# Spacing the weight buffers of parts 2 and 3 over 512 bytes (attention with sinks, then mixture of experts, fp32, one core)

## The chip, the cores and the metric

The kernel runs on one core of one Trainium2 chip. The metric is the time on the device in microseconds. The kernel before takes 2079.2 us, the median of 2 runs (2079.17 and 2079.23).

## The reference, cut to what matters

Attention with 4 sink tokens and a window of 128 gives `x` (3072 tokens, 512 wide). Then come 8 experts: two dense layers with a ReLU between them, and the sum over the experts, weighted by a matrix `P` that a few Sinkhorn steps make from a gate. Nearly all of the arithmetic is in the two products of the loop.

```python
def _moe_ref(x, w_gate, w1, w2):          # x 3072x512, w1 8x512x1024, w2 8x1024x512
    ...
    for e in range(E):
        h = np.maximum(x @ w1[e], 0.0)
        ye = h @ w2[e]
        out += P[:, e:e + 1] * ye
    return out.astype(np.float32)
```

## The kernel before

**Parts and units.** After the attention the 3072 tokens are worked through in three parts of 1024. The code counts them 0, 1, 2; parts 2 and 3 of the title are `part` 1 and 2, and they run the same code. A part goes over 32 units: 8 experts times 4 slices of 256 hidden columns (`units1`).

**Products.** fp32 values are split into a high and a low fp32r half, and three of the four cross products are kept. On top of that both layers use a fast matrix scheme with seven products M1 to M7 in place of eight, for which each unit's weights are kept in DRAM as seven ready "forms" (`w1s`, `w2s`), written during part 1. In parts 2 and 3 a unit's first layer is seven products of 6 matmuls each (`product`, L902: `c<-B,W1q` or `c<-T,W1q`). Its second layer takes units in pairs: 14 groups of 6 matmuls for a pair of units, one group a tick (L1467: `o<-hf,W2q` or `held<-hf,W2q`); in such a group a buffer of `W2q` is read by 3 matmuls in a row, in a product a buffer of `W1q` by 6. So a unit is 42 + 42 = 84 matmuls, all with 128x128 stationary weights and 512 moving columns.

**What is stationary, what moves.** In each matmul the stationary operand is 128 columns of a weight form, 512 bytes of a partition, out of a buffer `W1q` or `W2q`. The moving operand is 2048 bytes of a partition: of `XF` (the token forms B11 to T4) in the first layer, of `hf` (the hidden forms) in the second.

**Buffers and loads.** `W1q` has 8 buffers and `W2q` 16 (`W1N`, `W2N`), each 2048 bytes a partition, one form per buffer, used in turn. `load_w1` (L1350 to L1356) and `load_w2` (L1370 to L1376) put one DMA per form on SP's queue: 128 rows of 2048 bytes. A buffer is asked for again one tick after the last matmul that read it. The first four forms of part 2 come out of another pool (`WT`, `early_form`) and are no part of the change. Pools hand out addresses one buffer after the other, and in the built program all buffers named here begin at a multiple of 512 bytes: the `W1q` buffers at 76800, 78848, 80896 and so on, those of `W2q` from 196096 on, and all of `XF` and `hf` too.

**What sets the order.** The program stands in the order in which it is written (`manual_schedule`). `tick` runs what is due and then one product or one group of the second layer; `STEPS2` is the order of ticks in a unit.

Of the kernel before, what the change touches and what calls it, by code (L numbers as in the profile page):

```python
# [10 lines left out]
F32R = mybir.dt.float32r  # L11
# [5 lines left out]
P = 128  # L17
# [221 lines left out]
def tile_sink_attention_moe(ctx: ExitStack, tc: tile.TileContext, q, k, v, wg, w1, w2, out):  # L239
# [15 lines left out]
    KH = KC // 2  # L255
# [7 lines left out]
    def f32(ap):  # L263
        return ap.bitcast(F32)
# [118 lines left out]
    for hh in range(2):  # L383
        t = att2.tile([P, NP, CW + 2 * P], F32, name=f"KQF{hh}")
# [520 lines left out]
    HD = DM // 2  # L905
    weighted = []
    W1Q = {}
# [34 lines left out]
    w1p, cp, rawp, sp, xrp = (pool_(*a) for a in (("w1p", 1), ("cp", 1), ("rawp0", 2), ("sp", 2), ("xrp", 1)))  # L942
# [393 lines left out]
    with ExitStack() as p1:  # L1336
        pool_ = lambda name, bufs, **kw: p1.enter_context(tc.tile_pool(name=name, bufs=bufs, reuse_waits="tile", **kw))
        W1N, W2N = 8, 16
        w1p, pb, cp, wp, hp = pool_("w1q", W1N), pool_("pb", 2), pool_("cq", 1), pool_("wq", 6), pool_("hq", 16)
        ORDER = ["M2", "M1", "M5", "M3", "M6", "M7", "M4"]  # L1340
        units1 = [(e, u) for e in range(E) for u in range(NU)]
        NJ = len(units1)
# [3 lines left out]
        W2Q = {}  # L1346
        coming1 = iter([(part, n, m) for part, n in jobs1 for m in ORDER if (part, n, m) not in W1Q])
        first_ones = set(W1Q)

        def load_w1(k):  # L1350
            for _ in range(k):
                key = next(coming1, None)
                if key:
                    part, n, m = key
                    t = W1Q[key] = w1p.tile([P, 2, KH, P], F32R, name="W1q")
                    nc.sync.dma_start(f32(t).rearrange("p w k f -> p w (k f)"), w1s[units1[n]][:, FA[W1_OF[m]]])  # L1356

        W2_OF = {"M1": "B11", "M2": "B21", "M3": "B22", "M4": "T4", "M5": "T1", "M6": "T2", "M7": "T3"}
# [11 lines left out]
        def load_w2(k):  # L1370
            for _ in range(k):
                key = next(coming2, None)
                if key:
                    part, n, m = key
                    t = W2Q[key] = w2p.tile([P, 2, HD], F32R, name="W2q")
                    nc.sync.dma_start(f32(t), w2s[units1[n]][:, FORMS.index(W2_OF[m])])  # L1376

        PBS = {}
# [13 lines left out]
        def first2(part, n):  # L1392
# [4 lines left out]
            def run(m):  # L1397
                c = "c2" if m in ("M2", "M5", "M3") else "c1"
                start = m in ("M2", "M1", "M5")
                if start:  # L1400
                    T[c] = ps0.tile([P, HT], F32, name=c)
                W = W1Q.pop((part, n, m))
                product(T[c], lambda a, k: W[:, a, k, :], XF[READS[m]], start, True)
                if (part, n, m) not in first_ones:
                    at(1, lambda: load_w1(1))
                if (part, n) == (1, NJ - 1):
                    at(1, lambda: load_form(m))
# [48 lines left out]
        def second2(part, group):  # L1456

            begin, end = group[0] == 0, group[-1] == NJ - 1
            for m, k in order_of(group):
# [11 lines left out]
                def then(m=m, k=k, o=o, hold=hold):  # L1471
                    if hold:
                        sums[m, k] = o
                    elif end and (m, k) == ("M3", 1):
                        for cols in HALVES if part == 2 else (slice(0, HT),):
                            nc.vector.tensor_add(sums["M6", k][:, cols], o[:, cols], sums["M6", k][:, cols])
                    elif begin:
                        t = sums[m, k] = (accq if (m, k) in FEW else accp).tile([P, DM], F32, name="acc")
                        nc.scalar.copy(t, o)
                    else:  # L1480
                        nc.vector.tensor_add(sums[m, k], o, sums[m, k])  # L1481
                    if end:
                        together(part, m, k)
                        if (m, k) == ("M4", 1):
                            at(2 if part == 2 else 3, lambda: put_out(part, 1))
                        if part == 1 and (m, k) == ("M3", 1):
                            at(2, lambda: put_out(part, 0))
                        if part == 2 and m in ("M2", "M3"):

                            d = 2 * (m == "M3") + k  # L1490
                            at(1 if d == KC - 1 else 2, lambda d=d: last_out(d, ("c1", "c2", "held1", "held3")[d]))
                    if (m, k) != ("M3", 1) and k == 1 or (m, k) == ("M3", 0) and not end or (m, k) == ("M3", 1) and end:
                        at(1, lambda: load_w2(len(group)))
# [92 lines left out]
        def second_pools():  # L1586
            nonlocal w2p, accq
            p0r.close()
            w2p, accq = pool_("w2q", W2N, side="right"), pool_("accq", 3, side="right")
            load_w2(W2N)  # L1590

        w2p = accq = None
        load_weights(1, 0)
        load_w1(W1N)
        unit(1, 0, last_second, BEGIN[0])
        unit(1, 1, last_second, BEGIN[1][:-1] + [second_pools] + BEGIN[1][-1:])
# [46 lines left out]
```

## Time and profile before

| | |
|---|---|
| median of 2 runs | 2079.2 us |
| span of the profiled execution | 2077.3 us, so 1.9 us of the time lie outside it |
| PE (TensorE matmul) busy | 2060.9 us, 99% |
| PEld (TensorE weight load) busy | 1706.0 us, 82%, beside the matmuls |
| DVE, ACT, POOL busy | 70%, 40%, 34% |
| chain that ended last | 96% PE |
| granted TensorE clock | 0.999 of full speed, mean of the span |
| DMA | 453.78 MB moved, queue q1 busy for 69.6% of 16 engines' span |
| matmuls of `W1q` and `W2q` | 2664 and 2688 |

The page gives an engine's busy time, and for each group of instructions the line, the engine, what is written and read, the count and the mean duration. A matmul's duration there (389 ns for 512 columns) is longer than its share of the time, since matmuls overlap; the spacing of starts in the timeline is what counts. A row of the timeline merges neighbours of one line and gives the first one's start and the time from that start to the last one's end.

### The profile page before, as it was taken

How to read it: one execution, taken by the hardware profiler on the slowest of the kernel's cores; microseconds unless marked ns; L12 is line 12 of the kernel's file. 1: busy time of each engine (PE TensorE's matmuls, PEld its weight loads, DVE VectorE, ACT ScalarE, POOL GpSimd, SP SyncE). 2: the span in 40 equal slices, each digit the busy share in tenths (PEclk: the TensorE clock that was granted, in tenths of full speed). 3: DMA queues.
4: the chain of work that ended last, by engine and by line, in shares of the span. 5: the costliest groups of instructions: out<-in, count | busy, mean ns of one | idle time of the engine just before them, and what ended most of it. 6: DMA issues, size and time to landing. Idle time of an engine off the chain costs nothing.

```text
span 2077.3 us, 31257 instructions
## 1 busy us (share of the span) xinstructions
PE 2060.9 (99%) x10407; PEld 1706.0 (82%) x10407; DVE 1462.4 (70%) x2732; ACT 840.2 (40%) x1787; POOL 713.7 (34%) x833
## 2 busy tenths in 40 slices
PE   8999999999999999999999999999999999999998
PEld 7888778888888888888888888888888888888887
DVE  6777688787877767756666666666666667666666
ACT  7877445444444444333323322332432232333222
POOL 7766523333333321322322232233332223222323
PEclk9999999999999999999999999999999999999999
DMA  7655269898989886766666666668766666666662
GB/s 178 161 118 120 85 211 323 288 319 291 315 282 323 289 274 223 280 211 197 199 203 198 204 205 191 202 207 334 224 208 194 200 205 191 207 203 202 197 193 83
DMA packets 397622, 453.78 MB, mean 218 GB/s; under 512 B 99664, under 2 KB 265744, under 8 KB 396560
## 3 DMA queue, kind: packets, MB, share of 16 engines
q1 hardware_dynamic: 397064, 451.57, 69.6%
q8 instruction: 85, 1.39, 0.3%
q14 instruction: 81, 0.66, 0.1%
q10 hardware_dynamic: 392, 0.16, 0.0%
HBM read 314.17 MB, written 137.46 MB: 217 GB/s over the span
## 4 chain that ended last, share of the span: by engine, by line
PE 96%; DVE 2%; ACT 1%; POOL 0%; issue 0%; DMA 0%; SPq 0%; DVEq 0%; ACTq 0%; POOLq 0%
PE c L902 42%; PE o L1467 21%; PE held L1467 8%; PE held L1152 7%; PE o L1152 7%; PE st L638 2%; PE st L652 2%; PE st L572 2%; PE st L498 2%; PE st L457 1%; PE st L530 1%; PE st L580 0%; DVE sc L508 0%; DVE st L507 0%; PE st L603 0%
## 5 line engine op out<-in xcount | busy, mean ns | idle before, releaser
L928 ACT CAST hf<-w 128x512 fp32r<-128x512 f32 x448 | 265.3, 621 | 562.2 <-POOL w L1434 299.7
L1467 PE MATMUL o<-hf,W2q 128*128 128x512 f32 x1920 | 472.0, 389 | 0.0
L1467 PEld LDWEIGHTS o<-hf,W2q 128*128 128x128 f32 x1920 | 360.0, 188 | 75.5 <-DVE acc L1481 0.9
L902 PE MATMUL c<-T,W1q 128*128 128x512 f32 x1530 | 388.8, 389 | 0.2 <-DVE w L1415 0.2
L931 DVE TENSOR_TENSOR hf<-w,hf 128x512 fp32r<-128x512 f32 x448 | 329.1, 763 | 75.6 <-ACT hf L928 68.0
L902 PEld LDWEIGHTS c<-T,W1q 128*128 128x128 f32 x1530 | 286.8, 188 | 60.7 <-DVE w L1415 0.9
L1481 DVE TENSOR_TENSOR acc<-o,acc 128x512 f32<-128x512 f32 x298 | 204.6, 687 | 169.9 <-PE o L1467 169.9
L902 PE MATMUL c<-B,W1q 128*128 128x512 f32 x1134 | 278.3, 389 | 0.0
L1434 POOL TENSOR_TENSOR w<-w 128x512 f32<-128x512 f32 x64 | 82.7, 1293 | 492.0 <-DVE w L1416 492.0
L902 PEld LDWEIGHTS c<-B,W1q 128*128 128x128 f32 x1134 | 212.5, 188 | 44.0
L1415 DVE TENSOR_TENSOR w<-c,M 128x512 f32<-128x512 f32 x192 | 132.2, 689 | 139.9 <-PE c L902 135.6
L1411 ACT COPY M<-c 128x512 f32<-128x512 f32 x192 | 112.8, 587 | 249.1 <-PE c L902 249.0
L1467 PE MATMUL held<-hf,W2q 128*128 128x512 f32 x768 | 194.8, 389 | 0.0
L1152 PE MATMUL held<-W2f,h 128*128 128x512 f32 x672 | 171.1, 390 | 0.0
L902 PE MATMUL c<-T,W1f 128*128 128x512 f32 x672 | 171.0, 390 | 0.1
L1152 PE MATMUL o<-W2f,h 128*128 128x512 f32 x672 | 170.5, 389 | 0.1
L1467 PEld LDWEIGHTS held<-hf,W2q 128*128 128x128 f32 x768 | 144.0, 188 | 29.8
L1449 POOL TENSOR_TENSOR w<-w 128x512 f32<-128x512 f32 x64 | 106.3, 1661 | 176.0 <-DVE hf L931 176.0
L1152 PEld LDWEIGHTS o<-W2f,h 128*128 128x128 f32 x672 | 126.0, 188 | 27.0 <-DVE acc L1159 0.9
L902 PEld LDWEIGHTS c<-T,W1f 128*128 128x128 f32 x672 | 125.8, 188 | 26.9 <-issue 0.5
L1152 PEld LDWEIGHTS held<-W2f,h 128*128 128x128 f32 x672 | 125.8, 188 | 26.4 <-DVE W2f L931 0.5
L961 POOL TENSOR_TENSOR r<-r 128x256 f32<-128x256 f32 x27 | 20.1, 745 | 367.8 <-ACT M L1115 231.4
(216 smaller groups left out, 2740.3 us busy)
## 6 DMA issues: line engine op xcount, KB each, us to landing
W2q<-w2s SPq DMA_DIRECT2D x448, 256.0 KB, 3.1
W1q<-w1s SPq DMA_DIRECT2D x444, 256.0 KB, 2.8
w1s<-W1f SPq DMA_DIRECT2D x56, 896.0 KB, 7.7
w2s<-WT SPq DMA_DIRECT2D x136, 256.0 KB, 3.2
r<-in_moe_w_dram SPq DMA_DIRECT2D x64, 512.0 KB, 5.5
w2s<-W2f SPq DMA_DIRECT2D x56, 256.0 KB, 5.7
PB<-psd SPq DMA_DIRECT2D x16, 512.0 KB, 4.0
w2s<-W2f SPq DMA_DIRECT2D x56, 128.0 KB, 7.8
```

Of the source, the lines that this page charges most:

```text
L498: nc.tensor.matmul(ps[hh * HH + 2 * pr + r][:, 0:w], lhsT=Q[rows, a, pr, :], rhs=K[rows, c, pr, 0:w], start=(j == 0), stop=(j == len(terms ...
L572: nc.tensor.matmul(O[r * D:(r + 1) * D, c], lhsT=x_[:, 2 * c + r], rhs=y_[:, 2 * c + r], start=(j == 0 and c == 0), stop=(j == len(ops) - ...
L902: nc.tensor.matmul(ps, lhsT=w1(a, k), rhs=x[:, b, k, :], start=(start and j == 0), stop=(stop and j == len(TERMS) - 1), skip_group_check=n ...
L928: nc.scalar.copy(dst[:, 0], src)
L931: low_ = nc.vector.tensor_sub(dst[:, 1], src, f32(dst[:, 0])).ins
L1152: nc.tensor.matmul(o, lhsT=h[c, th][:, a, off:off + P], rhs=W2F[n][:, w, c, :], start=(begin and c == 0 and j == 0), stop=(end and c == 1 ...
L1411: nc.scalar.copy(t, T["c2"])
L1415: nc.vector.tensor_add(w, T["c1"], T[m])
L1434: nc.gpsimd.tensor_sub(S3, T["A11"], T["A21"])
L1449: at(k, lambda: nc.gpsimd.tensor_sub(T["A11"], w, T["A11"]))
L1467: nc.tensor.matmul(o, lhsT=W2Q[part, n, m][:, a, k * P:(k + 1) * P], rhs=F[part, n, H_OF[m]][:, w, :], start=(j == 0 and (begin or not hol ...
L1481: nc.vector.tensor_add(sums[m, k], o, sums[m, k])
```

## The change

Each of the two pools now hands out tiles that are longer than what is used: by 16 words (64 bytes) for `W1q` and by 8 words (32 bytes) for `W2q`. The form lies in the first 2048 bytes, and the rest is never touched. As the tiles follow each other, the eight `W1q` buffers begin at 0, 64, 128, ... 448 modulo 512 bytes, and the sixteen `W2q` buffers at 0, 32, 64, ... 480. The pools behind them move by 512 bytes in all, so `XF`, `hf` and the other tiles stay at multiples of 512.

```diff
+        def spaced(pool, gap, name):
+
+            return pool.tile([P, 2 * HD + gap], F32R, name=name)[:, 0:2 * HD]
+
...
-                    t = W1Q[key] = w1p.tile([P, 2, KH, P], F32R, name="W1q")
+                    t = W1Q[key] = spaced(w1p, 16, "W1q").rearrange("p (w k f) -> p w k f", w=2, k=KH)
                     nc.sync.dma_start(f32(t).rearrange("p w k f -> p w (k f)"), w1s[units1[n]][:, FA[W1_OF[m]]])
...
-                    t = W2Q[key] = w2p.tile([P, 2, HD], F32R, name="W2q")
+                    t = W2Q[key] = spaced(w2p, 8, "W2q").rearrange("p (w d) -> p w d", w=2)
                     nc.sync.dma_start(f32(t), w2s[units1[n]][:, FORMS.index(W2_OF[m])])
```

No instruction is added, taken away or moved on any engine; the lines behind the new function have numbers larger by 5. Since the pools' ends move by up to 512 bytes, a few of the first loads into fresh buffers wait for other instructions than before. On SP's queue, at the start of part 2, the load of the expert weights `PB` stands ahead of the first eight loads of `W1q`:

```order
 L1205 DMA WT<-w1s_4750 128x512 [waits DMAHW5_49,PE_49]
 L1205 DMA WT<-w1s_4750 128x512 [waits DMAHW6_49]
-L1383 DMA PB<-psd 128x1024 [waits DMAHW7_49,DVE_49]
-L1356 DMA W1q<-w1s_4750 128x512 [waits DMAHW0_49,PE_49]
-L1356 DMA W1q<-w1s_4750 128x512 [waits DMAHW1_49]
...
+L1388 DMA PB<-psd 128x1024 [waits DMAHW7_49,DVE_49,PE_49]
+L1361 DMA W1q<-w1s_4750 128x512 [waits DMAHW0_49,PE_49]
+L1361 DMA W1q<-w1s_4750 128x512 [waits DMAHW1_49]
```

The load of `PB` waits for a count of PE too now. In the built program that count is 2067, and the load of `W1q` right behind it in the same queue waits for 4359, before and now.

## Rows read from the trace of the kernel before

**Rows 1.** The page: span, busy time by engine, granted clock, chain by engine.
```profile
span 2077.3 us, 31257 instructions
...
PE 2060.9 (99%) x10407; PEld 1706.0 (82%) x10407; DVE 1462.4 (70%) x2732; ACT 840.2 (40%) x1787; POOL 713.7 (34%) x833
...
PEclk9999999999999999999999999999999999999999
...
PE 96%; DVE 2%; ACT 1%; POOL 0%; issue 0%; DMA 0%; SPq 0%; DVEq 0%; ACTq 0%; POOLq 0%
```

**Rows 2.** Chain in order of time, part 2: start, length, engine, line, count.
```profile
900.19 4.08 PE c L902 x18
919.23 4.08 PE c L902 x18
```

**Rows 3.** Waits of PE from 860 us on: total, times, longest.
```profile
PE c L902 <- DVE w L1415: 0.2, 1, 0.2
```

**Rows 4.** Stretch 900 to 1400 us: busy time by engine, clock, DMA share, GB/s.
```profile
900.00:1400.00 500.00, 500.00 (x2207) 414.02 (x2206) 339.28 (x500) 152.78 (x264) 146.33 (x105) 1.00 0.66 201
```

**Rows 5.** Page, groups of matmuls: line, out<-in, count | busy us, mean ns | idle.
```profile
L1467 PE MATMUL o<-hf,W2q 128*128 128x512 f32 x1920 | 472.0, 389 | 0.0
...
L902 PE MATMUL c<-T,W1q 128*128 128x512 f32 x1530 | 388.8, 389 | 0.2 <-DVE w L1415 0.2
...
L902 PE MATMUL c<-B,W1q 128*128 128x512 f32 x1134 | 278.3, 389 | 0.0
...
L1467 PE MATMUL held<-hf,W2q 128*128 128x512 f32 x768 | 194.8, 389 | 0.0
```

**Rows 6.** Timeline of matmuls, part 3: start, length, line, out<-in, count.
```profile
1602.34 1.52 PE L902 MATMUL c<-T,W1q 128*128 128x512 f32 x6
1603.70 1.52 PE L1467 MATMUL held<-hf,W2q 128*128 128x512 f32 x6
```

**Rows 7.** Timeline of weight loads at the same place, part 3.
```profile
1602.11 1.32 PEld L902 LDWEIGHTS c<-T,W1q 128*128 128x128 f32 x6
1603.47 0.64 PEld L1467 LDWEIGHTS held<-hf,W2q 128*128 128x128 f32 x3
```

**Rows 8.** Timeline of transposes in the attention stage (L457, L530).
```profile
97.16 0.27 PE L457 MATMUL st<-ident,kr 128*128 128x128 f32 x1
97.27 0.27 PE L457 MATMUL st<-ident,qr 128*128 128x128 f32 x1
97.37 1.04 PE L530 MATMUL st<-ident,sc 128*128 128x128 f32 x8
98.25 0.27 PE L554 MATMUL st<-ident,SS 128*96 128x128 f32 x1
```

**Rows 9.** Timeline of matmuls behind a set of transposes, part 3.
```profile
1465.68 1.64 PE L902 MATMUL c<-B,W1q 128*128 128x512 f32 x6
1467.16 1.53 PE L902 MATMUL c<-T,W1q 128*128 128x512 f32 x6
1468.52 1.52 PE L1467 MATMUL held<-hf,W2q 128*128 128x512 f32 x6
```

**Rows 10.** Timeline, cut from the second matmul behind another set of transposes.
```profile
1464.17 1.32 PE L1467 MATMUL o<-hf,W2q 128*128 128x512 f32 x5
1465.33 0.27 PE L1534 MATMUL o<-ident,acc 128*128 128x128 f32 x1
```

**Rows 11.** Groups by shape, 70 to 266 us: 512-column matmuls between attention's small ones.
```profile
L652 PE MATMUL st<-W2f,h 128*128 128x512 f32 x168 | 41.7, 397 | 0.0
L638 PE MATMUL st<-B,W 128*128 128x512 f32 x144 | 35.5, 396 | 0.3
```

**Rows 12.** Loads of `W1q` (L1356), from issue to landing.
```profile
DMA to landing us min/median/max: 2.5/2.8/9.3
```

**Rows 13.** Loads of `W2q` (L1376), from issue to landing.
```profile
DMA to landing us min/median/max: 2.5/3.1/6.9
```

## The prediction

> **What bounds the kernel now.** I read the page first. TensorE has matmuls under way for 2060.9 of the 2077.3 us, and the chain that ended last is PE for 96% [rows 1]. The other engines are at 70% and below, so a microsecond saved or lost there shows only where PE waits for it. Next the chain in order of time: in part 2 it comes back in the same piece every unit, 900.19 and 919.23 us, 19.04 us apart [rows 2]. Then the waits: from 860 us to the end PE has one wait that the profile sees, 0.2 us long [rows 3]. So in parts 2 and 3 nothing but PE's own pace counts.
>
> That pace is very even. The stretch from 900 to 1400 us is filled by 2207 matmuls, two of them cut by its edges: 500 / 2206 = 226.7 ns from start to start [rows 4]. A unit gives the same, 19.04 us / 84 = 226.7 ns [rows 2], and so does a product or a group: six matmuls between 1602.34 and 1603.70 us [rows 6]. The granted clock is 1.00 in that stretch [rows 4], the 2.4 GHz level. 512 columns at one column a cycle of that clock would be 213.3 ns. So each matmul carries 13.3 ns beyond its columns, 32 cycles, and no wait that the trace names. This is what the change can touch.
>
> The weight loads lie beside the matmuls. The load for the matmul of 1602.34 us begins at 1602.11, which is when the matmul before it begins (1602.34 less 0.227) [rows 6, 7]. Load and moving stream of two neighbouring matmuls thus start together, and before the change they start at the same place modulo 512 bytes. The load is over well before the next start.
>
> **The change, part by part.** How many matmuls read a moved buffer: 1920 + 768 from `W2q`, 1530 + 1134 from `W1q`, 5352 in all [rows 5]. At 226.7 ns they are 1213 us of the time. One nanosecond more or less on each is 5.35 us. A change by 2% of 2079.2 us, 41.6 us, would need 7.8 ns on every one. (Two per cent is about what a measurement of this kernel can tell from no change.)
>
> *Instructions and loads.* None is added or moved. The load of `PB` waits for an earlier PE count than the `W1q` load right behind it waits for anyway, and nothing stands between them in the queue: 0. The DMAs move the same 2048 bytes a row to places that are no longer multiples of 512. If they take longer, their cover is the depth of the buffers: `W1q` has 8 for 7 products a unit, so a load has 8/7 of 19.04 us, 21.8 us, less the one or two ticks (1.4 us each [rows 6]) until it is issued. `W2q` has 16 for the 14 forms of two units, 16/14 of 38.1 us, 43.5 us. They land in 2.8 and 3.1 us by the median, in 9.3 and 6.9 at worst [rows 12, 13]. Even twice the worst is covered: 0. At the very start of `W2q` the first loads are close to their use, and there a microsecond could be lost once.
>
> *The load of weights from an uneven place.* The nearest rows are the transposes of the attention stage, which are so short (128 columns, 53 ns at that clock, against 0.11 us from one to the next) that the loads set their pace. Those of L457 read raw tiles in steps of 512 bytes and follow each other by 0.11 us. Those of L530 read `sc` in steps of 528 bytes (132 words a head), so that each lies 16 bytes further on modulo 512 than the last: eight in 98.25 - 97.37 = 0.88 us, 0.11 us each [rows 8]. A load that begins at any multiple of 16 bytes takes the same time there. In parts 2 and 3 the load is hidden behind 512 columns besides. Taken alone: 0.
>
> *How load and moving stream meet.* This is the open item. All 512-column matmuls of this trace have both operands at a multiple of 512, so none shows another meeting. From below: if the 13.3 ns come wholly from that meeting and vanish, 5352 x 13.3 = 71 us are gained, 2008 us. From above: the even pace is lost. Behind a set of transposes it is lost for a moment, and the next six matmuls take 1.48 us in place of 1.36 [rows 9]; without the first, which also waits for its weights, five take 1465.33 - 1464.17 = 1.16 us, 232 ns each [rows 10]. If all 5352 went so, they would cost 5.3 ns x 5352 = 28 us more. In the stretch where 512-column matmuls stand between attention's small ones their mean duration is 396 to 397 ns, 7 to 8 above the 389 of parts 2 and 3 [rows 5, 11]; 8 ns x 5352 = 43 us is my upper end, 2122 us. Between these ends I take 0, by the row that is nearest to the operation that the change moves: weight loads at places that differ from one to the next [rows 8] kept their time.
>
> The sum: 0 for the loads, 0 for the order, 0 for the pace; span 2077.3 us, with the 1.9 us outside it 2079.2 us, the median of the runs.
>
> **The rivals.** *Faster: load and moving stream get in each other's way.* For it speaks that they start together and at the same place modulo 512 bytes, and that 13.3 ns have no other name in the trace. Spaced buffers would meet the stream elsewhere; one W1 buffer in 8 and one W2 buffer in 16 stay at 0. Against it: the moving stream runs over 2048 bytes while the load runs over 512, so it passes the load's place modulo 512 whatever the start is, and I see no start that avoids this altogether. No row has the size, so I take the middle between nothing and all: 6.7 ns, 5352 x 6.7 = 36 us, 2043 us. From 7.8 ns on it is over 2%.
>
> The Trainium skill (TensorE: Matmul & The Clock Gate, Back-to-back issue gap) gives N/2.4 + 2.5 ns at the full clock, 215.8 ns for 512 columns. The rows show 226.7, 10.9 more. If the spacing brought the page's pace, the estimate would be 58 us less, 2021 us; no run here shows such a pace yet.
>
> *Slower: the even pace depends on equal places.* Matmuls fall back to 226.7 ns only one product behind a disturbance: at 1467.16 us the next product takes 1.36 us again [rows 9]. So the pace is a state that needs some six matmuls to be reached. Buffers change every six matmuls in the first layer, every three in the second. If each change of place disturbs the state, it is never reached, and all 5352 go at 232 ns: 28 us, 2108 us. Against it: now too the operands change all the time, only by multiples of 512, and nothing disturbs the pace; nor do the other engines' accesses at that time. It is over 2% only where a disturbed matmul takes 234.5 ns and more.
>
> *The transfers to uneven places become the bound.* For it: 0.66 of the DMA engines' time is taken in part 2 [rows 4]. Against it: a cover of 20 us against landings of 3. If they took half as long again the share would be near 1; then PE would wait somewhere, and I put the price at 20 us, 2099 us, without a row for it.
>
> The Trainium skill (DMA: Bandwidth & Descriptors, How a descriptor splits into AXI transactions) says that a piece that does not begin at a multiple of 256 bytes is cut at the boundary below it. By its table's rule a row of 2048 bytes at 64 would be an estimated 66 beats in place of 64. That speaks against the change, by 3% of a landing, far inside the cover; no row here has such a piece apart from others.
>
> **How the numbers follow.** No effect 0.50. Slower by a disturbed pace 0.25, of that 0.06 beyond 2%. Faster by a better meeting 0.22, of that 0.08 beyond 2%. Transfers 0.03, within 2%. The time is that of the likeliest, 2079.2 us. Below 2043 us lie about 0.10 (the upper half of the faster rival), above 2108 us about 0.09 (the worse half of the slower one); the range is 2043 to 2108, which holds the rest, and the likeliest case alone has 2077 to 2081. Faster by over 2% 0.08, within 2% 0.86, slower by over 2% 0.06.
>
> **What would show it.** Right: the chain's pieces of 18 matmuls at 4.08 us, units 19.04 us apart, rows of six at 1.36 us. The faster rival: rows of six at 1.32 us or less in the timeline, at the same clock, and all the more for buffers far from 0. The slower one: rows of six at 1.38 to 1.41 us, in both layers, and mean durations above 389 ns. The transfers: landings well above 3 us, a DMA share near 1, and waits of PE for `W1q` or `W2q`. I would be wrong in the main step if the 13.3 ns turn out to depend on where the weights lie; then the transposes were the wrong row to go by, since a 128-column matmul is over before its moving stream can meet much of the next load.

## The result

The changed kernel takes 2105.99 us (2105.86 and 2106.12) against 2079.2 us: 26.8 us more. The ratio is 1.0129, 95% interval 1.0099 to 1.0158. That is within 2%, and clearly slower. The forecast was no change, with a range of 2043 to 2108 us; the time lies near the range's upper end, almost where the slower rival had put it (2108).

The page of the changed kernel, to be held against [rows 1, 5]:

```profile
span 2104.1 us, 31256 instructions
...
PE 2088.1 (99%) x10407; PEld 1706.5 (81%) x10407; DVE 1466.7 (70%) x2732; ACT 839.8 (40%) x1787; POOL 712.5 (34%) x833
...
L1472 PE MATMUL o<-hf,W2q 128*128 128x512 f32 x1920 | 482.4, 395 | 0.0
...
L902 PE MATMUL c<-T,W1q 128*128 128x512 f32 x1530 | 395.7, 394 | 0.2 <-DVE w L1420 0.2
...
L902 PE MATMUL c<-B,W1q 128*128 128x512 f32 x1134 | 283.7, 394 | 0.0
...
L1472 PE MATMUL held<-hf,W2q 128*128 128x512 f32 x768 | 199.0, 395 | 0.0
```

PE's counts are the same, and the total of the weight loads hardly moved (1706.5 us against 1706.0). What grew and counts is PE, by 27.2 us, nearly all of it in the four groups that read the moved buffers: their mean duration went from 389 to 394 and 395 ns. Next the chain in order of time, the stretch from 900 to 1400 us, the timeline of part 3, PE's waits, and the landings of the `W1q` loads and of the `W2q` loads:

```profile
920.72 4.18 PE c L902 x18
940.20 4.18 PE c L902 x18
```

```profile
900.00:1400.00 500.00, 500.00 (x2158) 405.02 (x2157) 332.54 (x488) 149.37 (x258) 141.09 (x102) 1.00 0.65 196
```

```profile
1634.29 1.56 PE L902 MATMUL c<-T,W1q 128*128 128x512 f32 x6
1635.69 2.95 PE L1472 MATMUL o<-hf,W2q 128*128 128x512 f32 x12
1638.48 1.55 PE L902 MATMUL c<-T,W1q 128*128 128x512 f32 x6
```

```profile
PE c L902 <- DVE w L1420: 0.2, 1, 0.2
```

```profile
DMA to landing us min/median/max: 2.6/2.8/9.5
DMA to landing us min/median/max: 2.6/3.1/7.1
```

A unit is 19.48 us long (940.20 less 920.72), where it was 19.04 [rows 2]. The stretch holds 2158 matmuls for 2207 [rows 4], 231.8 ns each. Six matmuls take 1.40 us (1634.29 to 1635.69) for 1.36 [rows 6], in both layers. The clock is 1.00 as before, PE has the same one wait [rows 3], and the loads land as they did [rows 12, 13]. So the matmuls that read the moved buffers are on average about 5.1 ns slower, and 5352 x 5.1 = 27 us is the whole loss. Nothing waits for anything that the trace names. What remains to be found is what a matmul has to do with the place of its weights.

### The profile page after: what moved, and what is told of

It reads as the page before. It is cut to its first block, busy times and chain, and to the rows that moved or that the text cites. A ratio compares the mean times of both kernels' runs of the same rounds, so it can differ in the third digit from the quotient of the medians.

```text
span 2104.1 us, 31256 instructions
## 1 busy us (share of the span) xinstructions
PE 2088.1 (99%) x10407; PEld 1706.5 (81%) x10407; DVE 1466.7 (70%) x2732; ACT 839.8 (40%) x1787; POOL 712.5 (34%) x833
## 4 chain that ended last, share of the span: by engine, by line
PE 96%; DVE 2%; ACT 1%; POOL 0%; issue 0%; DMA 0%; SPq 0%; DVEq 0%; ACTq 0%; POOLq 0%
PE c L902 42%; PE o L1472 21%; PE held L1472 8%; PE held L1152 7%; PE o L1152 7%; PE st L638 2%; PE st L652 2%; PE st L572 2%; PE st L498 2%; PE st L457 1%; PE st L530 1%; DVE sc L508 0%; PE st L580 0%; DVE st L507 0%; PE st L603 0%
## 5 line engine op out<-in xcount | busy, mean ns | idle before, releaser
L1472 PE MATMUL o<-hf,W2q 128*128 128x512 f32 x1920 | 482.4, 395 | 0.0
L902 PE MATMUL c<-T,W1q 128*128 128x512 f32 x1530 | 395.7, 394 | 0.2 <-DVE w L1420 0.2
L902 PE MATMUL c<-B,W1q 128*128 128x512 f32 x1134 | 283.7, 394 | 0.0
```

Of the source, the lines that this page charges most:

```text
L902: nc.tensor.matmul(ps, lhsT=w1(a, k), rhs=x[:, b, k, :], start=(start and j == 0), stop=(stop and j == len(TERMS) - 1), skip_group_check=n ...
L1472: nc.tensor.matmul(o, lhsT=W2Q[part, n, m][:, a, k * P:(k + 1) * P], rhs=F[part, n, H_OF[m]][:, w, :], start=(j == 0 and (begin or not hol ...
```

## Experiments

Three theories were held against each other. *Changes*: the even pace breaks because the place changes from buffer to buffer (the slower rival of the prediction). *Distance*: what counts is how far the weights lie from the moving tile (the weights' address less the moving tile's, modulo some number of bytes), whether that changes or not. *Place*: the address of the weights counts by itself.

### One place for all buffers: const64

Both pools get their old tiles back, and a small pool ahead of each (and one behind, so that all others stay) puts all 24 buffers at 64 modulo 512. `lead` opens a pool with one tile of so many words of 4 bytes, which nothing reads.

```diff
-        w1p, pb, cp, wp, hp = pool_("w1q", W1N), pool_("pb", 2), pool_("cq", 1), pool_("wq", 6), pool_("hq", 16)
+        lead("lead1", 16)
+        w1p = pool_("w1q", W1N)
+        lead("lead2", 112)
+        pb, cp, wp, hp = pool_("pb", 2), pool_("cq", 1), pool_("wq", 6), pool_("hq", 16)
...
+            lead("lead3", 112, side="right")
+            w2p = pool_("w2q", W2N, side="right")
+            lead("lead4", 16, side="right")
```

> All eight W1q buffers and all sixteen W2q buffers begin at 64 modulo 512 bytes, none at 0, and the place does not change from buffer to buffer; moving tiles stay at 0. Theory of changes (what breaks the even pace is that the place changes every three to six matmuls): the pace settles again at 226.7 ns, about 2079 us. Theory of distance (a load 64 bytes away from the place at which the moving stream begins meets it badly, every time): matmuls that load from 64 went at about 233 ns in the changed kernel, so 5352 x 6.4 ns = 34 us more, about 2113 us. Rival without either (the spacing costs through the pools' other addresses): about 2106 us as in the changed kernel.

It took 2113.78 us, ratio 1.0167 (1.0150 to 1.0184): 34.6 us more than before, and more than the changed kernel. Timeline of part 3:

```profile
1605.58 2.96 PE L1474 MATMUL o<-hf,W2q 128*128 128x512 f32 x12
1608.38 1.56 PE L902 MATMUL c<-T,W1q 128*128 128x512 f32 x6
1609.78 1.56 PE L1474 MATMUL held<-hf,W2q 128*128 128x512 f32 x6
```

Twelve matmuls in 2.80 us and six in 1.40 are 233.3 ns each, again very even, without any change of place. The theory of changes falls as the main cause: an unchanging place can be worse than many places.

### Places 256 bytes apart: w1_256

```diff
-                    t = W1Q[key] = w1p.tile([P, 2, KH, P], F32R, name="W1q")
+                    t = W1Q[key] = spaced(w1p, 64, "W1q").rearrange("p (w k f) -> p w k f", w=2, k=KH)
```

> W1q buffers alternate between 0 and 256 modulo 512 bytes (gap of 64 words), W2q stays at 0. Theory of changes: the place changes at every product, so 2664 matmuls lose 5.3 ns, 14 us, about 2093 us, more if the groups between them are disturbed too. Theory of distance with a period of 256 bytes (in the changed kernel matmuls that load from 0 and 256 had the same mean, 230 ns, and so had 64 and 320): no loss, about 2079 us.

2079.05 us, ratio 0.9999 (0.9990 to 1.0009). The place changes at every product, by 256 bytes, and nothing is lost. Timeline of part 3, and the stretch from 900 to 1400 us:

```profile
1606.49 1.52 PE L902 MATMUL c<-T,W1q 128*128 128x512 f32 x6
1607.85 1.52 PE L1472 MATMUL o<-hf,W2q 128*128 128x512 f32 x6
```

```profile
900.00:1400.00 500.00, 500.00 (x2208) 414.19 (x2207) 339.53 (x500) 152.65 (x264) 146.13 (x105) 1.00 0.65 201
```

2208 matmuls in the stretch, where it was 2207 [rows 4]. So 256 bytes are as good as 0. In the trace of the changed kernel, too, the `W1q` buffers that lie 256 bytes apart have nearly the same mean spacing (233.1 ns at both 64 and 320, 232.4 and 232.1 at 128 and 384). The effect repeats after 256 bytes, and the W1 buffers of the change stood at four different places, not eight.

### Weights and moving tiles together: all64, and all tiles but the weight buffers: mov64

The first tile of the left side and of the right side of the memory are lengthened and shortened by 64 bytes, which moves every tile behind them by 64. In mov64 the weight buffers are put back with pools like those of const64.

```diff
-    const.tile([P, 8], F32, name="pad")
+    const.tile([P, 24], F32, name="pad")
...
-    base.tile([P, 120], F32, name="base")
+    base.tile([P, 104], F32, name="base")
```

> Everything on both sides of the memory moves by 64 bytes, stationary and moving tiles alike, in all parts; weights and moving tiles keep their distance of 0 modulo 512. If only the distance between the two counts: about 2079 us. If the place of the weights itself counts (64 is bad whatever moves): at least the 34 us of const64, about 2113 us, and more for the matmuls of part 1, which move too.

> As all64, but the W1q and W2q buffers are put back to 0 modulo 512 while the moving tiles of parts 2 and 3 lie at 64. If the distance counts, the weights are now 64 bytes ahead of the moving tile, as at 192 and 448 in the changed kernel, where matmuls had a mean of 230 ns: 5352 x 3.4 ns = 18 us more, about 2097 us, or any settled pace of that distance. If the place of the weights counts alone: about 2079 us, unless part 1 has moved by itself, which all64 shows.

all64 took 2079.28 us, ratio 1.0002 (0.9992 to 1.0011); mov64 2091.14 us, ratio 1.0058 (1.0042 to 1.0075). The same stretch of all64, then of mov64:

```profile
900.00:1400.00 500.00, 500.00 (x2207) 414.12 (x2207) 339.25 (x500) 152.94 (x264) 146.13 (x105) 1.00 0.66 201
```

```profile
900.00:1400.00 500.00, 500.00 (x2186) 410.25 (x2186) 336.12 (x495) 151.07 (x261) 144.87 (x104) 1.00 0.65 199
```

With everything at 64 the pace is the old one: the place of the weights by itself does not count, and neither does the uneven place that the loads write to. With the weights at 0 and the moving tiles at 64 it is 228.9 ns (500 / 2185 = 228.8). So the distance between the two is what counts, and it has a sign: weights 64 bytes higher than the moving tile modulo 256 give 233.3 ns, weights 64 lower (a distance of 192) 228.9.

In mov64 the tiles of the other engines move along with the moving tiles, so a meeting of the weights with those engines' accesses is a rival. The traces speak against it. From 880 us on, 329 matmuls in each kernel have DVE, ACT and POOL idle from the start of the matmul before them to the start of the next: their mean spacing (without gaps over 250 ns) is 226.7 ns in the kernel before, 233.4 in const64 and 229.3 in mov64, nearly as that of all the others (226.7, 233.3 and 228.9). The expectation of 2097 us for mov64 was too high; it had taken the mean at 192 and 448 bytes in the changed kernel, 230 ns, for the settled pace.

### Every distance: scan16 and scan4

The buffers are longer by 256 bytes, and where the form begins in them depends on the expert, so that each of the 16 pairs of expert and part has one distance: it grows by `STEP` words, 4 (16 bytes) in scan16 and 1 (4 bytes) in scan4. `W2q` has 14 buffers in these two, to make room.

```diff
+        def spaced(pool, part, n, name):
+
+            d = STEP * ((part - 1) * E + units1[n][0])
+            return pool.tile([P, 2 * HD + 64], F32R, name=name)[:, d:d + 2 * HD]
```

> The form's place inside longer buffers (2304 bytes) goes up by 16 bytes from expert to expert: W1q and W2q both lie 0, 16, 32 ... 112 bytes from the moving tile's place modulo 256 in part 2 and 128 ... 240 in part 3, each for 4 units, 76 us at the even pace; W2q has 14 buffers in place of 16. Theory of distance: every expert runs at a settled pace of its own, 226.7 ns at 0, 233.3 at 64 and 229 at 192 as in the runs at these distances, and the whole is slower than before, about 2100 us. Theory of changes: the place is the same for 336 matmuls in a row, so all experts run at 226.7 ns, about 2079 us. The faster rival of the prediction needs at least one distance with rows of six below 1.36 us.

> The same with steps of 4 bytes, distances 0 to 60 bytes. If the memory is read in pieces of 64 bytes from the matmul's start on, the pace changes between 0 and 64 step by step and is 226.7 ns at 0 alone. If only multiples of some bytes count (16 or 32), the pace is a staircase. About 2090 to 2110 us by either; 2079 us if distances under 64 bytes do nothing.

scan16 took 2105.23 us, scan4 2108.31, beside 2079.37 for the kernel before. Some of the stretches of scan16 in which both layers read from one distance, in the order of time 16, 64, 176, 192 and 208 bytes, PE alone (their first 2 to 3 us still hold groups of the second layer at the distance before):

```profile
935.00:975.00 40.00, 40.00 (x178) 1.00 0.63 197
...
1170.00:1210.00 40.00, 40.00 (x173) 1.00 0.63 188
...
1722.00:1762.00 40.00, 40.00 (x175) 1.00 0.62 190
1799.00:1839.00 40.00, 40.00 (x176) 1.00 0.63 191
1876.00:1916.00 40.00, 40.00 (x173) 1.00 0.62 191
```

The stretch of scan4 at 4 bytes, with its first 4 us still partly at 0:

```profile
935.00:975.00 40.00, 40.00 (x174) 1.00 0.64 191
```

The mean spacing from start to start in scan16, worked out from the starts in the trace, over the 144 to 236 matmuls of each distance whose neighbours on both sides read from it too:

| distance, bytes | ns | distance, bytes | ns |
|---|---|---|---|
| 0 | 226.7 | 128 | 233.3 |
| 16 | 226.8 | 144 | 233.3 |
| 32 | 233.3 | 160 | 233.4 |
| 48 | 233.3 | 176 | 230.0 |
| 64 | 233.4 | 192 | 229.0 |
| 80 | 232.0 | 208 | 233.4 |
| 96 | 234.2 | 224 | 233.3 |
| 112 | 233.3 | 240 | 226.9 |

In steps of 4 bytes (scan4) it is 226.8 at 0, 232.4 at 4, 230.7 at 8, 233.2 at 12, and from there to 60 between 229.8 and 235.0. Three things follow. In scan16 only 0 and its neighbours 16 and 240 keep the old pace, but at 16 scan4 shows 233.3 where scan16 shows 226.8, so there are two settled paces at that distance: the distance alone does not fix the pace everywhere. In scan16 the matmuls ahead of that stretch stood at 0, in scan4 at 12; whether this is the reason was not tried. No distance goes below 226.7 ns: the faster rival falls for every constant place that was tried. And the table accounts for most of the loss of the change: W1 stood at distances 0, 64, 128 and 192 in equal shares, mean 230.6, W2 at multiples of 32, mean 232.1; 2664 x 3.9 + 2688 x 5.4 = 25 us of the 26.8. The pace in scan4 goes neither step by step nor as a staircase, the two pictures of its expectation: it jumps at 4 bytes and goes up and down behind that.

### One layer at a time: w1_only and w2_only

Of the two pools only the one named is spaced, as in the change.

> Only the W1q buffers are spaced, by 64 bytes; W2q stays at 0. By the settled paces of scan16 and const64 at 0, 64, 128 and 192 bytes (226.7, 233.3, 233.3, 229.0 ns, each place a quarter of the loads) the 2664 matmuls of W1q would go at 230.6 ns: 10 us more, 2090 us. If the changes of place cost something besides, it is more; if the groups of W2q between the products bring the pace back, less.

> Only the W2q buffers are spaced, by 32 bytes; W1q stays at 0. By the settled paces of scan16 at 0, 32 ... 224 bytes (226.7, 233.3, 233.3, 234.2, 233.3, 233.4, 229.0, 233.3 ns) the 2688 matmuls of W2q would go at 232.1 ns: 14 to 15 us more, 2094 us. The two losses should add up to the 27 us of the changed kernel within a few microseconds.

w1_only: 2092.66 us, ratio 1.0065 (1.0048 to 1.0081). w2_only: 2101.27 us, ratio 1.0107 (1.0090 to 1.0124). Both lost more than expected, 13.5 us for 10 and 22.1 for 14 to 15, and together 35.6, more than the change itself. The groups of the buffers that stayed at 0, first `W2q` in w1_only, then `W1q` in w2_only:

```profile
L1472 PE MATMUL o<-hf,W2q 128*128 128x512 f32 x1920 | 474.1, 390 | 0.0
...
L1472 PE MATMUL held<-hf,W2q 128*128 128x512 f32 x768 | 195.9, 391 | 0.0
```

```profile
L902 PE MATMUL c<-T,W1q 128*128 128x512 f32 x1530 | 392.5, 392 | 0.2 <-DVE w L1420 0.2
...
L902 PE MATMUL c<-B,W1q 128*128 128x512 f32 x1134 | 281.2, 392 | 0.0
```

They are slower too, 390 to 392 ns where 389 was the mean at distance 0 [rows 5]. From the starts in the trace they go at 227.9 ns (W2 in w1_only) and 229.2 (W1 in w2_only). This is the second, smaller effect: behind matmuls at another distance those at 0 do not have their pace at once. In w1_only the six W2 matmuls behind a product at distance 64 follow each other by 231, 231, 236, 228, 232 and 231 ns on average, and those after them by 226.7; behind a product at 128 only the first takes 231, and behind one at 0 none is slower. This is also why the two losses do not add up. The buffers at 0 lose 2688 x 1.2 = 3 us in w1_only and 2664 x 2.5 = 7 us in w2_only; that leaves 10 and 15 us for the spaced buffers themselves, as expected, and 25 to 26 us together. The expectation for w1_only had named such a cost without a size, the one for w2_only had left it out.

### Another order of the columns: turns16 and turns32

scan16 again, with the 512 columns of each matmul taken in turns from their two halves, 16 or 32 at a time, both where they are read (`rhs`) and where the result is written (`o`).

```diff
+        def turns(t):
+
+            return t.rearrange("p (a b c) -> p b a c", a=2, c=16)
...
-                    nc.tensor.matmul(o, lhsT=W2Q[part, n, m][:, a, k * P:(k + 1) * P], rhs=F[part, n, H_OF[m]][:, w, :],
+                    nc.tensor.matmul(turns(o), lhsT=W2Q[part, n, m][:, a, k * P:(k + 1) * P], rhs=turns(F[part, n, H_OF[m]][:, w, :]),
```

> As scan16 (distance 0 to 240 bytes in steps of 16, one distance per expert and part), and the 512 columns of each matmul of parts 2 and 3 are read, and written, in another order: 16 columns (64 bytes) of the first half, 16 of the second half, the next 16 of the first, and so on; the result stands in the same places. The halves lie 1024 bytes apart, so modulo 256 bytes the moving stream now goes half as fast. If the 13.3 ns beyond the columns come from the places at which the two streams meet modulo 256 bytes, the pace by distance changes altogether, and some distance should let them never meet: a pace below 226.7 ns, down to 216 or so. If the 13.3 ns are a fixed cost of each matmul and the distance only adds to it, no distance goes below 226.7 ns.

> The same with 32 columns (128 bytes) from each half in turn. Meeting of streams: the table by distance differs from that of scan16 and of turns16, with some distance below 226.7 ns. Fixed cost: the best distance stays at 226.7 ns.

turns16 took 2149.41 us, turns32 2126.84, beside 2079.05. Timeline of turns16 in part 2:

```profile
970.68 1.60 PE L1476 MATMUL held<-hf,W2q 128*128 128x512 f32 x6
972.12 1.60 PE L902 MATMUL c<-T,W1q 128*128 128x512 f32 x6
973.56 3.04 PE L1476 MATMUL o<-hf,W2q 128*128 128x512 f32 x12
```

1.44 us for six is 240.0 ns, and it is 240.0 at all sixteen distances. In turns32 the pace is 233.3 at 32, 96, 208 and 224 bytes, 240.0 at 80, and between 235.6 and 237 at the others; at 0, the best distance of scan16, it is 236.7. So the order of the columns sets the pace as well, and it changes what a distance costs. Whether the order of reading or that of writing does it is not separated by these two runs. But no combination went below 226.7 ns, and in the new orders none below 233.3. The idea that some order lets load and stream never meet, and frees the 13.3 ns, found no support; that the 13.3 ns are a fixed cost is not shown by it either, since the new order brought a cost of its own. The other half of the expectation for turns32, that the best distance stays at 226.7 ns, did not come true either.

No run beat the kernel before; w1_256 and all64 equal it.

## Why the prediction was right or wrong

**What bounds the kernel: right.** PE's pace in parts 2 and 3 was the one thing that could move, and it alone moved. 5352 matmuls, 5.35 us a nanosecond: 5.1 ns gave 27 us.

**Instructions, order, loads: right.** The landings stayed, PE's waits stayed, the DMA share stayed, and the later wait of the `PB` load cost nothing that shows.

**The load from an uneven place: right, and beside the point.** The loads' total duration did not change. I took this row as the nearest for the open item.

**How load and moving stream meet: this is the step that failed.** I had both ends, 2008 and 2122 us, and the pace of disturbed matmuls, 232 ns; the changed kernel goes at 231.8. But I took 0, "by the row that is nearest to the operation that the change moves", and put the disturbed pace with a rival. In place of 0 the runs show 5.1 ns on the mean matmul of the change: its pace depends on how far the weights lie from the moving tile modulo 256 bytes, 233.3 ns with all weights 64 bytes off (const64) and the old pace when both move (all64). The transposes of [rows 8] did not show the effect. Their pace is set by the load, and the load's recorded duration is not what changed: it is 188 ns in the changed kernel and in const64 as before, and the spacing of 512-column matmuls grew beside it. That a 128-column matmul is too short to show the effect is argued, as at the end of the prediction, and not tested. The better row was [rows 10]: it showed that a 512-column matmul can take more than 226.7 ns with no wait and at the same clock, so that 226.7 was no fixed cost.

**The size of noise: wrong.** I held that two per cent is about what a measurement of this kernel can tell from no change. The two runs of each kernel lie within 0.3 us of each other, and 26.8 us stands far outside that. The time lies within my range only because the range reached up to the slower rival; the sum behind 2079.2 us has no part in that.

**The slower rival: right size, wrong main cause.** It had 2108 us, from 232 ns a matmul. Its mechanism was that changes of place break the pace. That the change came out near its figure is luck: the mean over the distances that these gaps happen to give, 231.8 ns, happens to lie near the pace of a stream behind transposes, 232. Const64 has no changes and loses 34.6 us; w1_256 changes place at every product and loses nothing. The main cause is the distance modulo 256 bytes, with a settled pace at each (two at 16 bytes). The part of it that holds is the second effect: a matmul at distance 0 loses 1.2 to 2.5 ns on average when its neighbours stand elsewhere (w1_only, w2_only), which fits the several matmuls that the pace needs to settle [rows 9].

**The faster rival: refuted as far as tried.** I argued that the stream passes the load's place whatever the start is, and that no start avoids it. The scan agrees: no distance below 226.7 ns. But the argument would have made all starts alike, and they are not.

**Transfers: refuted,** 2.8 and 3.1 us as before.

What stays open is the mechanism inside: why the pace of a stream of 2048 bytes beside a load of 512 depends on the distance between them, whether the two wait for each other at all, and what the 13.3 ns at distance 0 are.

## What to carry to other kernels

Where TensorE is the bound and every matmul loads new weights, look at the spacing of starts in the timeline: an even spacing above the columns' time can depend on where the stationary tile lies against the moving one, and the trace names no wait for it. In this kernel no distance that was tried beat a multiple of 256 bytes, and pads that look harmless cost 1.3%. A row of an operation with another bound is no evidence, however close the operation looks.

## What the runs showed of the hardware that I had not expected

- For 512-column fp32r matmuls that each load 128 columns of weights, the pace depends on the distance between the two operands modulo 256 bytes: 226.7 ns at 0, 233.3 at most others, 229 at 192 (const64, mov64, scan16; in w1_256 256 bytes are as 0), at a granted clock of 1.00, the 2.4 GHz level.
- A distance of 4 bytes is enough: 232.4 ns (scan4).
- Three settled paces stand out, 6.67 ns apart, which is 16 cycles of that clock: 226.7, 233.3 and 240.0 (before, const64, turns16). They are not the only ones: scan16 has 229.0, 230.0, 232.0 and 234.2 too. A settled pace can be a cycle of a few values, as 226, 229 and 232 ns in turn in the starts of mov64, or 231 and 236 in parts of const64.
- A stream at distance 0 behind a product at 64 takes six matmuls to come back to 226.7 ns (w1_only).
- The load itself shows next to nothing of it: 188 ns in the page of every one of these kernels but turns16, where it is 191.
- The same 512 columns, read and written 16 at a time from two halves in turn, take 240.0 ns at every distance of scan16 (turns16).
